# Attention and a Fourier gate on one core: tables from bit operations, transposes in halves, a new order, and matmuls of zeros

## The chip, the core and the metric

The kernel runs on one core of a Trainium2 chip. A core has five engines that work side by side, each through its own list of instructions in order: PE (matrix multiplication, results in the accumulator memory PSUM), DVE (vector work), ACT (functions and copies), POOL (general vector work, and the issue of some transfers) and SP (which only issues transfers). Transfers (DMA) are carried by 16 DMA engines which all queues share. Engines wait for one another through semaphores. The metric is the time of one launch in microseconds (us), the median of several runs; smaller is better.

## The reference

The inputs q, k and v have 8 batches, 8 heads, 576 positions and 64 numbers each. The first stage is a linear attention with a feature map of 2 x 128 features; the second takes its output as `x` (8 x 576 x 512), projects it to three parts, convolves the second over the positions by a Fourier transform, multiplies the three and projects once more.

```python
def phi(x):
    proj = np.einsum('bhsd,df->bhsf', x, w_phi)
    proj = proj - np.max(np.abs(proj), axis=-1, keepdims=True)
    return np.concatenate([np.exp(proj), np.exp(-proj)], axis=-1)
q_p, k_p = (phi(q), phi(k))
kv = np.einsum('bhsf,bhsd->bhfd', k_p, v)
z = np.sum(k_p, axis=2)
num = np.einsum('bhsf,bhfd->bhsd', q_p, kv)
den = np.einsum('bhsf,bhf->bhs', q_p, z)[..., None] + 1e-06
x = num / den                       # heads side by side: 8 x 576 x 512
proj = x @ w_proj                   # 512 x 1536
x1, x2, x3 = proj[..., :D], proj[..., D:2 * D], proj[..., 2 * D:]
X2 = np.fft.rfft(x2, n=S, axis=1)
H = np.fft.rfft(filter_fft, n=S, axis=0)[None, :, :]
x2_conv = np.fft.irfft(X2 * H, n=S, axis=1)
return (x1 * x2_conv * x3) @ w_out
```

## The kernel before

All work is written as a list of words, PLAN (lines 24 to 172), which `run` (line 850) reads from the first to the last. A word is the name of a method, its arguments and, behind `@`, the PSUM bank. `Pk,1,2@0` calls `Pk(1, 2)` on bank 0. Every method issues its instructions on fixed engines, so the order of the words is the order on each engine, and nothing else sets it. Where two engines touch the same buffer, the framework adds the wait. The first number of most words is the batch, 0 to 7. Buffers stand in rings (RING, line 20); two batches of q, k and v fit at once.

One batch takes this way. `load` (line 473) brings q, k or v from memory through POOL's queue, changing float32 to bf16. `tr` (line 485) transposes k or q with a DMA from SP; for batch 0 `loadh` and `trh` (lines 479 and 489) do it in halves. `Pk`, `Qn` and the tails `Pkt`, `Qnt` multiply with `w_phi` on PE (lines 504 to 529), `maxk` and `maxq` take the largest absolute value on DVE (line 576), `ex` the exponentials on ACT (line 560). For q the maxima are cut into a bf16 part (`mhi` on ACT) and the rest (`mlo` on DVE, line 601), transposed (`trm`, line 605, into `mT`) and subtracted within `Pq` by matmuls with the table `sel` (line 543). `em` and `vs` (lines 610 and 616) scale v on POOL, `KV` and `NE` (lines 631 and 652) are the two products of the attention on PE, `rc` and `xn` divide on DVE (lines 666 and 671), and `trx` and `trxt` (lines 690 and 695) transpose the result from SP into `xT` and `xTt`.

From `xT` the second stage begins: `X1` and `X3` (line 750) are projections on PE, as are `X1t` and `X3t` for the tail. `fold` and `foldt` (lines 707 and 713) add and subtract halves of the positions on POOL, `X2` (line 719) projects them, `F` (line 408) is the forward transform as matmuls with the table `fwd`, `m1`, `m2` and `m3` multiply with the filter's transform (tables `A`, `B`), `I` (line 798) is the inverse transform with the table `inv`, `ym` multiplies the parts, `O` (line 830) is the last projection and `st` stores from SP. While one batch is in the second stage the next is in the first; PLAN interleaves them.

Ahead of that the first batch needs tables. The angles of the Fourier tables come from rows that POOL's `iota` writes (`gen_rows`, line 271) and DVE's constants (`gen_phase`); 30 float32 matmuls turn them into columns (`gen_cols`, lines 312 and 314), DVE makes angles of them (`gen_angles`, lines 332 to 335), ACT sines (`gen_sin`). DVE writes the five-part tables (`gen_five`, line 353), `sel` (`gen_sel`, lines 465 to 469) and `inv` (`gen_inv`). Six DMA transposes (`gen_fwd`, line 363) make `fwd`, `fwd5` and `fwdh`. The filter is loaded in 20 pieces from SP (`filt_load`, lines 383 and 385), folded on POOL (`filt_fold`, lines 390 to 393), and `H` with `H_ev` makes `A` and `B`.

The DMAs of a queue share eight semaphores in turn: a DMA on SP waits until the one eight places before it on SP has landed, and so on POOL's queue. POOL waits in its place in the list, so the vector work behind a waiting load waits too.

Of the kernel before, what the change touches and what calls it, by code (L numbers as in the profile page):

```python
# [25 lines left out]
gen_sin loadh,k,0,0 filt_load,SP,0 w_load,phi w_phi trh,q,0,1 Qn,0,3@0 trh,q,0,0 hold,q,0 trh,k,0,0
trh,k,0,1 Qn,0,2@2 maxq,0,2@2 load,k,1 maxq,0,3@0 Qn,0,1@4 maxq,0,1@4 Pk,0,0@2 ex,k,p,0,0@2 Qn,0,0@6
Pk,0,2@0 ex,k,p,0,2@0 ex,k,m,0,2@0 filt_load,SP,1 Qnt,0@4 maxqt,0@4 maxq,0,0@6 Pk,0,1@4 ex,k,p,0,1@4
zeros mhi,0 ex,k,m,0,0@2 gen_selidx gen_five gen_sel Pkt,0@6 exkt,p,0@6 exkt,m,0@6 gen_fwd,3
load,v,0 gen_fwd,0 mlo,0 maxk,0,2@0 trm,0 Pk,0,3@0 load,q,1 ex,k,p,0,3@0 ex,k,m,0,3@0 maxk,0,0@2  # L30
Pq,0,2@2 maxk,0,1@4 ex,k,m,0,1@4 maxkt,0@6 em,p,0,0 em,m,0,0 maxk,0,3@0 tr,k,1 em,p,0,1 gen_fwd,1
Pq,0,1@4 load,v,1 filt_fold H,3@0 H_ev,DVE,3@0 Pq,0,0@6 ex,q,m,0,1@4 ex,q,p,0,1@4 ex,q,p,0,0@6
ex,q,m,0,0@6 H,0@1 H_ev,DVE,0@1 vs,p,0,0 em,m,0,1 ex,q,p,0,2@2 vs,m,0,0 vs,m,0,1 Pq,0,3@4 Pqt,0@0
tr,q,1 KV,0,0@6 KVe,DVE,0,0@6 exqt,p,0@0 gen_inv exqt,m,0@0 NE,0,0@6 rc,0,0@6 ex,q,m,0,2@2 Pk,1,2@0
xn,0,0@6 Pkt,1@2 exkt,p,1@2 exkt,m,1@2 Pk,1,3@6 maxk,1,2@0 ex,q,m,0,3@4 maxkt,1@2 maxk,1,3@6
gen_fwd,5 ex,q,p,0,3@4 em,m,1,1 vs,p,0,1 KV,0,1@2 ex,k,p,1,2@0 KVe,DVE,0,1@2 gen_fwd,2 NE,0,1@4
w_load,proj,0 rc,0,1@4 xn,0,1@4 ex,k,m,1,2@0 w_load,proj,1 gen_fwd,4 ex,k,p,1,3@6 vs,m,1,1 NE,0,2@2
rc,0,2@2 xn,0,2@2 NEt,0@4 rct,0@4 w_load,proj,2 Qn,1,1@0 maxq,1,1@0 xnt,0,1@4 w_load,proj,3 NE,0,3@2
xnt,0,0@4 trxt,0 Qnt,1@0 em,p,1,1 rc,0,3@2 xn,0,3@2 Pk,1,1@4 ex,k,m,1,3@6 ex,k,m,1,1@4 Qn,1,2@6
maxq,1,2@6 H,2@2 H_ev,ACT,2@2 maxqt,1@0 H,1@3 trx,0,3 vs,p,1,1 Qn,1,0@6 maxq,1,0@6 H_ev,ACT,1@3  # L40
trx,0,1 maxk,1,1@4 Qn,1,3@0 trx,0,2 H_fix H,4@2 H_ev,ACT,4@2 maxq,1,3@0 late foldt,0,1 KV,1,1@6
ex,k,p,1,1@4 Pk,1,0@2 X3t,0@4 trx,0,0 X1t,0@5 X1te,ACT,0@5 foldt,0,0 X2,0,4@0 X3,0,3@5 X1,0,3@1
mhi,1 KVe,DVE,1,1@6 mlo,1 maxk,1,0@2 em,p,1,0 load,k,2 X2e,ACT,0,4@0 em,m,1,0 trm,1 X1,0,2@6
X1e,ACT,0,2@6 fold,0,1 X2,0,2@0 X2e,DVE,0,2@0 load,q,2 tmt,0@4 X2,0,3@7 ex,k,p,1,0@2 load,k,3
X2e,DVE,0,3@7 X1,0,1@6 X1,0,0@4 X1e,DVE,0,0@4 ex,k,m,1,0@2 X1e,ACT,0,1@6 F,0,3@0 fold,0,0 X2,0,1@6
X1e,ACT,0,3@1 tm,0,3@5 X2e,DVE,0,1@6 Pqt,1@2 X2,0,0@1 exqt,m,1@2 exqt,p,1@2 X2e,DVE,0,0@1 F,0,2@6
Fe,DVE,0,2@6 Pq,1,0@4 ex,q,p,1,0@4 ex,q,m,1,0@4 vs,p,1,0 Fe,DVE,0,3@0 vs,m,1,0 F,0,1@1 Fe,DVE,0,1@1
# [847 lines left out]
```

## Time and profile before

| What | Value |
|---|---|
| median of 3 runs | 376.44 us (373.03 to 376.76) |
| profiled execution, its own time | 378.21 us |
| profiled execution, span | 376.4 us |
| PE busy | 303.6 us, 81% of the span |
| DVE, POOL, ACT busy | 273.8, 241.2, 219.1 us |
| DMA queue of SP and ACT, share of 16 engines | 38.3% |
| DMA queue of POOL, share of 16 engines | 28.4% |
| read from and written to memory | 33.88 and 9.44 MB |

The span runs from the first to the last instruction that the profile shows; the execution's own time is 1.8 us longer. "Busy" counts the time in which an engine had an instruction under way. In the rows that follow, a row of the timeline gives its start, its length, engine, line, operation and tiles, and in brackets how long the engine had stood idle before and what ended that. A row of stretches gives the stretch, its length, the busy time (and number of instructions) of PE, PE's weight loads, DVE, ACT and POOL, the clock granted to PE as a share of full speed, the busy share of the DMA engines and GB/s. A row of the chain gives start, length and what the chain of waits was in. A row of waits names who waited for whom, the total, how often and the longest.

### The profile page before, as it was taken

Reading aid. Unit: us, or ns where it says so; the run is one execution under the profiler, and the core shown is the slowest. Engines: PE = TensorE matmul, PEld = TensorE weight load, DVE = VectorE, ACT = ScalarE, POOL = GpSimd, SP = SyncE. Lnnn points to the kernel's source line nnn. Section 1 sums busy time; section 2 is a strip of 40 time slices with the busy share of each in tenths; the row PEclk is TensorE's granted clock in tenths of the full one; section 3 lists DMA queues with packets and bytes.
Section 4 is the critical chain, followed back from the end, with each engine's and each line's share of the span. In section 5 each row is a group of like instructions: output and inputs, shape, how many; then the busy total and the mean of one; then the engine's idle time right before and its main releaser. Section 6 shows DMA issues by size and latency. Waiting matters only on the chain.

```text
span 376.4 us, 9310 instructions
## 1 busy us (share of the span) xinstructions
PE 303.6 (81%) x3816; PEld 171.1 (45%) x3863; DVE 273.8 (73%) x450; ACT 219.1 (58%) x346; POOL 241.2 (64%) x184
## 2 busy tenths in 40 slices
PE   5230757599939999798699998699897999999993
PEld 5220345335614565355344664247442664564451
DVE  3759678527947899688577799959885798767860
ACT  1153766436736787467456877567674857763342
POOL 5408455296674998687387766783789478856440
PEclk9999988979979999999879999989998999999998
DMA  8998489794998698667949363536706271223226
GB/s 165 179 210 116 78 127 165 118 178 70 147 168 142 108 95 141 140 114 134 186 75 215 73 108 80 99 64 93 152 4 124 51 135 33 60 51 70 57 63 161
DMA packets 82171, 42.82 MB, mean 114 GB/s; under 512 B 63440, under 2 KB 76368, under 8 KB 82128
## 3 DMA queue, kind: packets, MB, share of 16 engines
q1 hardware_dynamic: 68320, 25.97, 38.3%
q0 software_dynamic: 13808, 16.25, 28.4%
q8 instruction: 30, 0.49, 0.5%
q14 instruction: 13, 0.11, 0.1%
HBM read 33.88 MB, written 9.44 MB: 115 GB/s over the span
## 4 chain that ended last, share of the span: by engine, by line
PE 61%; DMA 18%; DVE 11%; issue 4%; SPq 2%; ACT 2%; POOL 0%; DVEq 0%; ACTq 0%; POOLq 0%
PE ps L750 14%; PE ps L719 9%; PE ps L408 8%; PE ps L830 6%; DMA qT<-qn 6%; PE ps L631 5%; DMA xT<-xn 5%; PE ps L652 4%; PE ps L798 4%; DMA kT<-kn 3%; PE ps L543 2%; DMA qn<-in_q_dram 2%; PE ps L537 2%; PE ps L516 2%; DMA mT<-mh 2%
## 5 line engine op out<-in xcount | busy, mean ns | idle before, releaser
L750 PE MATMUL ps<-xT,wproj 128*128 128x512 bf16 x244 | 69.1, 408 | 10.7 <-DMA xT<-xn 9.8
L576 DVE TENSOR_REDUCE mq<-ps 128x8 f32<-128x1024 f32 (+1 forms) x40 | 43.5, 1111 | 22.8 <-PE ps L523 12.1
L818 POOL TENSOR_TENSOR yT<-cv,x1s 128x576 bf16<-128x576 f32 x25 | 32.4, 1315 | 25.6 <-DVE cv L807 19.1
L616 POOL TENSOR_TENSOR vm<-vn,vm 128x1152 bf16<-128x1152 bf16 x16 | 34.4, 2152 | 20.4 <-ACT vm L610 20.4
L737 POOL TENSOR_TENSOR t<-C,B 128x512 bf16<-128x512 bf16 x32 | 36.4, 1154 | 14.5 <-ACT C L636 7.2
L707 POOL TENSOR_TENSOR eo<-xT 128x1024 bf16<-128x1024 bf16 x16 | 35.0, 2196 | 16.1 <-DMA xT<-xn 9.9
L576 DVE TENSOR_REDUCE mk<-ps 128x8 f32<-128x1024 f32 (+1 forms) x40 | 43.7, 1110 | 2.1 <-PE ps L523 0.6
L616 POOL TENSOR_TENSOR vp<-vn,vp 128x1152 bf16<-128x1152 bf16 x16 | 34.4, 2152 | 12.5 <-ACT vp L610 8.8
L408 PE MATMUL ps<-x2n,fwd 128*128 128x512 bf16 (+1 forms) x121 | 38.2, 387 | 4.7 <-DVE x1s L638 3.0
L750 PEld LDWEIGHTS <-wproj 128*128 128x128 bf16 x256 | 23.6, 103 | 39.0 <-issue 14.6
L560 ACT ACTIVATE Ekp<-ps 128x1024 bf16<-128x1024 f32 x32 | 32.8, 1030 | 14.5 <-PE ps L509 13.2
L830 PE MATMUL ps<-wout,yT 128*128 128x512 bf16 x132 | 36.8, 396 | 3.1 <-ACT x1s L636 1.4
L719 PE MATMUL ps<-wproj,eo 128*128 128x512 bf16 x154 | 39.0, 383 | 0.4 <-issue 0.2
L560 ACT ACTIVATE Eqm<-ps 128x1024 bf16<-128x1024 f32 x32 | 32.4, 1025 | 10.0 <-PE ps L543 10.0
L560 ACT ACTIVATE Eqp<-ps 128x1024 bf16<-128x1024 f32 x32 | 32.9, 1028 | 6.9 <-PE ps L543 6.3
L560 ACT ACTIVATE Ekm<-ps 128x1024 bf16<-128x1024 f32 x32 | 32.8, 1029 | 5.3 <-PE ps L509 4.8
L636 ACT CAST x1s<-ps 128x512 bf16<-128x512 f32 (+1 forms) x32 | 17.2, 547 | 29.7 <-PE ps L750 22.0
L745 POOL TENSOR_TENSOR Y<-Y,t 128x1024 bf16<-128x1024 bf16 x14 | 29.7, 2125 | 2.2 <-DVE Y L733 0.9
L733 DVE TENSOR_TENSOR Y<-ps,A 128x512 bf16<-128x512 f32 x40 | 26.6, 682 | 5.4 <-PE ps L408 5.2
L509 PE MATMUL ps<-wphi,kT 64*128 64x128 bf16 x256 | 14.2, 231 | 18.3 <-DVE mk L576 8.8
L807 DVE TENSOR_TENSOR cv<-es,ps 128x288 f32<-128x288 f32 x64 | 25.4, 447 | 4.2 <-ACT es L802 2.3
L798 PE MATMUL ps<-inv,Y 128*128 128x288 bf16 x192 | 28.3, 291 | 0.0
(142 smaller groups left out, 643.6 us busy)
## 6 DMA issues: line engine op xcount, KB each, us to landing
out_dram<-o SPq DMA_DIRECT2D x72, 128.0 KB, 2.4
vn<-in_v_dram POOLq DMA_DIRECT2D x8, 576.0 KB, 7.3
kn<-in_k_dram POOLq DMA_DIRECT2D x7, 576.0 KB, 8.5
qn<-in_q_dram POOLq DMA_DIRECT2D x7, 576.0 KB, 7.5
wproj<-in_moe_w_proj_dram POOLq DMA_DIRECT2D x4, 384.0 KB, 7.0
fl<-in_moe_filter_fft_dram SPq DMA_DIRECT2D x20, 64.0 KB, 5.2
kn<-in_k_dram POOLq DMA_DIRECT2D x2, 288.0 KB, 5.7
qn<-in_q_dram POOLq DMA_DIRECT2D x2, 288.0 KB, 6.8
```

The source lines that it names most:

```text
L408: self.mm(self.pb(0), l, r, start=(i == 0), stop=(i == len(ks) - 1))
L560: self.nc.scalar.activation(e, self.db(), AF.Exp, bias=0.0, scale=1.0 if g == "p" else -1.0)
L576: self.nc.vector.tensor_reduce(out=out, in_=src, axis=AX.X, op=ALU.max, apply_absolute_value=True)
L616: self.nc.gpsimd.tensor_tensor(out=t[:, :, :, 0:64], in0=self.at("vn", b)[:, 2 * X:2 * X + 2], in1=t[:, :, :, 64:65].to_broadcast([128, 2, ...
L707: self.nc.gpsimd.tensor_tensor(out=o, in0=x[:, :, :, 0, :], in1=x[:, :, :, 1, :], op=op)
L719: self.mm(self.pb(0), eo[:, kt, 128 * c:128 * c + 128], w[:, kt, 512:1024], start=(kt == 0), stop=(kt == 3))
L737: self.nc.gpsimd.tensor_tensor(out=self.at("t2", b)[:, t, :], in0=self.at("C", b)[:, t ^ 1, :], in1=self.at("B")[:, t, :], op=ALU.mult)
L745: e.tensor_tensor(out=Y, in0=Y, in1=self.at("t2", b)[:, s, :], op=ALU.add)
L750: self.mm(self.pb(0), w[:, kt, f0 + 128 * m:f0 + 128 * m + 128], x[:, kt, :], start=(kt == 0), stop=(kt == 3))
L798: self.mm(self.pb(e, 0, 288), Y[:, t, 128 * m:128 * m + 128], inv[:, e, i, :], start=(i == 0), stop=(i == 2))
L818: e.tensor_tensor(out=self.at("yT", b)[:, m, 0:SEQ], in0=self.at("cv", 4 * b + m).rearrange("p j h t -> p (j h t)"), in1=self.at("x1s", b) ...
L830: self.mm(self.pb(0), y[:, kt, 128 * j:128 * j + 128], w[:, kt, :], start=(kt == 0), stop=(kt == 3))
```

## The change

Four things are changed, and with them every position in PLAN.

The tables. The 30 matmuls, `gen_phase` and three iotas are gone; two iotas of one column each, shifts and masks on DVE give the columns (`gen_cols`, in two parts). The products of angle and column move from DVE to ACT (`gen_turns`), the reduction to whole turns stays on DVE in two parts. `gen_five`, `gen_sel`, `gen_inv` and the padding zeros move from DVE to POOL. The six transposes for the tables become two (`gen_fwd` with 12 blocks, `gen_fwd5` with 10). The filter's last row is loaded once a half instead of twice; one half goes through POOL's queue, the other through SP's. `mlo` moves to POOL for the batches 1 to 7.

The transposes. k and q of all batches are transposed in two halves by `trh`: 32 DMAs where there were 18.

The weights. `w_proj` is loaded by the three blocks of its columns in the order 2, 0, 1 (x3, x1, x2), where it was by four blocks of rows.

The matmuls of zeros. `warm,n` issues n matmuls of a zero tile with 512 columns into a bank whose content is not used; there are 48 in all: 22, 11, 2, 4, 2, 4, 1 and 2, the last of them in the middle of the second batch.

```diff
-gen_phase loadh,k,0,1 loadh,q,0,1 loadh,q,0,0 gen_rows gen_half gen_cols@0 gen_cols_ev@0 gen_angles
+w_load,phi w_phi zeros loadh,q,0,0 loadh,q,0,1 gen_rows loadh,k,0,0 trh,q,0,0 warm,22@0 Qn,0,0@0
+gen_cols,1 gen_turns,1 gen_cols,0 gen_turns,0 gen_angles,1 Qn,0,1@2 gen_angles,0 maxq,0,0@0
...
+    def warm(self, n):
+        z = self.at("idle")
+        for _ in range(n):
+            self.mm(self.pb(0).rearrange("p (i x) -> p i x", i=4), z,
+                    z.rearrange("p (i x) -> p i x", i=1).to_broadcast([128, 4, 128]), True, True)
...
-        g.iota(fr[:, 0:4, :], pattern=[[1, 2], [0, 2], [2, 128]], base=0, **kw)
+        g.iota(part, pattern=[[0, 1]], base=0, channel_multiplier=1, **kw)
+        g.iota(even, pattern=[[0, 1]], base=0, channel_multiplier=2, **kw)
...
+        for i in range(3):
+            v.tensor_scalar(out=bit[:, i:i + 1], in0=self.part, scalar1=4 + i, scalar2=1,
+                            op0=ALU.logical_shift_right, op1=ALU.bitwise_and)
+        v.tensor_scalar(out=bit[:, 3:4], in0=self.part, scalar1=15, scalar2=None,
+                        op0=ALU.bitwise_and)
+        v.tensor_copy(fb, bit)
...
+    def gen_turns(self, i):
+        cols = self.at("cols")
+        for t in (range(0, 4), range(4, 7))[i]:
+            self.nc.scalar.activation(self.turn[:, t, :], self.sc, AF.Identity,
+                                      bias=cols[:, 8 + t:9 + t], scale=cols[:, t:t + 1])
+
+    def gen_angles(self, i):
+        v = self.nc.vector
+        r = (slice(0, 4), slice(4, 7))[i]
+        t, w = self.turn[:, r, :], self.whole[:, r, :]
+        v.tensor_copy(w, t)
+        v.tensor_tensor(out=t, in0=t, in1=w, op=ALU.subtract)
...
     def gen_five(self):
-        v, m = self.nc.vector, self.at("msk")
+        g, m = self.nc.gpsimd, self.at("msk")
...
-    def gen_fwd(self, t):
...
+    def gen_fwd(self):
+        self.nc.sync.dma_start_transpose(
+            out=self.at("fwd").rearrange("p t c x -> p (t c) x"),
+            in_=self.G.rearrange("p t x -> p (t x)"))
...
     def gen_inv(self):
-        v, inv, m = self.nc.vector, self.at("inv"), self.at("msk")
+        v, inv, m = self.nc.gpsimd, self.at("inv"), self.at("msk")
...
-        q = self.nc.sync if eng == "SP" else self.nc.scalar
+        q = dict(SP=self.nc.sync, ACT=self.nc.scalar, POOL=self.nc.gpsimd)[eng]
...
-        for e in range(2):
-            q.dma_start(out=self.fl[i][32 * e:32 * e + 32, 2, :], in_=rows[8])
-
-    def filt_fold(self):
+        q.dma_start(out=self.fl[i][0:32, 2, :], in_=rows[8])
+
+    def filt_fold(self, i):
...
-            g.dma_start(out=self.at("wproj")[:, kt, :],
-                        in_=self.dram["w_proj"][128 * kt:128 * kt + 128, :])
+            c = slice(512 * kt, 512 * kt + 512)
+            g.dma_start(out=self.at("wproj")[:, :, c],
+                        in_=self.dram["w_proj"][:, c].rearrange("(t p) f -> p t f", p=128))
...
     def gen_sel(self):
-        v, idx = self.nc.vector, self.selidx
+        g, idx = self.nc.gpsimd, self.selidx
...
+    def gen_selx(self):
+        self.nc.gpsimd.tensor_copy(self.at("sel"), self.one[:, 0, :].rearrange(
...
-    def mlo(self, b):
+    def mlo(self, eng, b):
...
+        e = self.nc.vector if eng == "DVE" else self.nc.gpsimd
+        e.tensor_tensor(out=m[:, :, 1, 0:18], in0=self.at("mq", b),
+                        in1=m[:, :, 0, 0:18], op=ALU.subtract)
```

Three places show how the order moves. On DVE, near the first maxima of q and k, this stood before; `selone` and `sel` are the steps of the table `sel`, `mh` is the parted maximum that `trm` transposes, `mk` the maxima of k:

```order
L355 TENSOR_SCALAR G_154<-g_156,msk_74 128x32
L465 TENSOR_SCALAR selone<-selidx 128x18 x4
L467 TENSOR_TENSOR selone<-selone 128x36
L468 TENSOR_TENSOR selone<-selone 128x18
L469 CAST sel_63<-selone 128x2304
L601 TENSOR_TENSOR mh_88<-mq_86,mh_88 128x2x18
L576 TENSOR_REDUCE mk_84<-ps 128x2x4 x3
```

On DVE the same place now begins with the two parts of the angles and holds nothing of `sel` or of the five-part table `G`:

```order
L352 CAST whole<-turn 128x864
L353 TENSOR_TENSOR turn<-turn,whole 128x864
L352 CAST whole<-turn 128x1152
L353 TENSOR_TENSOR turn<-turn,whole 128x1152
L599 TENSOR_REDUCE mq_86<-ps 128x2x4 x3
L599 TENSOR_REDUCE mq_86<-ps 128x2x2
L599 TENSOR_REDUCE mq_86<-ps 128x2x4
L599 TENSOR_REDUCE mk_84<-ps 128x2x4
L625 TENSOR_TENSOR mh_88<-mq_86,mh_88 128x2x18
```

What moved is the building of `G` and `sel`, which has left the place between the maxima of q and `mh`.

On POOL, from the loads of batch 1 to the first scaling of v (`vp`, `vm`), this stood before:

```order
L474 DMA kn_78<-in_k_dram 128x4x576
L458 IOTA selidx 128x18
L474 DMA vn_79<-in_v_dram 128x4x576
L474 DMA qn_76<-in_q_dram 128x4x576
L474 DMA vn_80<-in_v_dram 128x4x576
L390 TENSOR_TENSOR fe<-fl_203,fl_204 128x512
L391 TENSOR_TENSOR fe<-fl_203,fl_204 128x512
L393 TENSOR_TENSOR fe<-fl_203,fl_204 32x512
L390 TENSOR_TENSOR fe<-fl_203,fl_204 128x512
L391 TENSOR_TENSOR fe<-fl_203,fl_204 128x512
L393 TENSOR_TENSOR fe<-fl_203,fl_204 32x512
L616 TENSOR_TENSOR vp_103<-vn_79,vp_103 128x18x64
```

On POOL now, behind nine pieces of the filter and the eight instructions of `gen_five`:

```order
L485 TENSOR_SCALAR selone<-selidx 128x18 x4
L487 TENSOR_TENSOR selone<-selone 128x36
L488 TENSOR_TENSOR selone<-selone 128x18
L497 DMA vn_79<-in_v_dram 128x4x576
L492 COPY sel_63<-selone 128x2304
L497 DMA kn_78<-in_k_dram 128x4x576
L497 DMA qn_76<-in_q_dram 128x4x576
L640 TENSOR_TENSOR vp_103<-vn_79,vp_103 128x18x64
L640 TENSOR_TENSOR vm_117<-vn_79,vm_117 128x18x64
L640 TENSOR_TENSOR vp_104<-vn_79,vp_104 128x18x64
L519 COPY junk_71<-qT_81 1x1
L640 TENSOR_TENSOR vm_118<-vn_79,vm_118 128x18x64
```

The filter's six folds (`fe`) now stand behind the scaling of v, the loads of batch 1 behind `sel`, and the load of v for batch 1 (`vn_80`) has gone further down.

On SP, from the transposes of k of batch 0 to the first `xT`, this stood before:

```order
L490 DMA_TRANSPOSE kT_82<-kn_77 128x9x128 x2
L383 DMA fl_204<-in_moe_filter_fft_dram 32x512 x8
L385 DMA fl_204<-in_moe_filter_fft_dram 32x512 x2
L363 DMA_TRANSPOSE fwd_66<-G 128x3x128 x2
L605 DMA_TRANSPOSE mT_90<-mh_88 128x128
L486 DMA_TRANSPOSE kT_83<-kn_78 128x18x128
L363 DMA_TRANSPOSE fwd_66<-G 128x3x128
L486 DMA_TRANSPOSE qT_81<-qn_76 128x18x128
L363 DMA_TRANSPOSE fwdh_68<-G_154 128x5x128
L363 DMA_TRANSPOSE fwd_66<-G 128x3x128
L363 DMA_TRANSPOSE fwd_67<-G_154 128x5x128
L695 DMA_TRANSPOSE xTt_133<-xnt_129 128x2x128
```

On SP now:

```order
L513 DMA_TRANSPOSE kT_82<-kn_77 128x9x128 x2
L402 DMA fl_142<-in_moe_filter_fft_dram 32x512 x8
L403 DMA fl_142<-in_moe_filter_fft_dram 32x512
L378 DMA_TRANSPOSE fwd_66<-G 128x12x128
L629 DMA_TRANSPOSE mT_90<-mh_88 128x128
L513 DMA_TRANSPOSE kT_83<-kn_78 128x9x128 x2
L383 DMA_TRANSPOSE fwd_67<-G_145 128x10x128
L513 DMA_TRANSPOSE qT_81<-qn_76 128x9x128 x2
L714 DMA_TRANSPOSE xT_131<-xn_128 128x4x128
L719 DMA_TRANSPOSE xTt_133<-xnt_129 128x2x128
L714 DMA_TRANSPOSE xT_131<-xn_128 128x4x128 x3
```

The first half of the filter, which stood at SP's very start, now stands behind the four transposes of batch 0, and the halves of batch 1 and the tables go in fewer, larger DMAs ahead of `xT`.

More of the change, by code (lines that the diff above doesn't have):

```diff
@@ L24 @@
 PLAN = """
-gen_phase loadh,k,0,1 loadh,q,0,1 loadh,q,0,0 gen_rows gen_half gen_cols@0 gen_cols_ev@0 gen_angles
[L26 to L47, printed above, removed]
@@ L216, in alloc @@
         R("junk", [1, 1], BF16)
+        R("idle", [128, 128], BF16)
         R("cols", [128, 16], FP32)
```

437 lines of the change are left out of this document (225 added, 212 removed).

## The prediction, made before the changed kernel ran

> **What bounds the kernel now.** I read the page first. PE is busy longest, but its slices show where it is not:
>
> ```profile
> span 376.4 us, 9310 instructions
> PE   5230757599939999798699998699897999999993
> ```
>
> One digit is 9.4 us. PE is idle or half idle in the first eight slices (75 us), and later in a few single ones. The same by stages, cut at the first matmul of the second stage:
>
> ```profile
> 0.00:74.50 74.50, 34.32 (x558) 25.97 (x561) 50.31 (x91) 34.34 (x52) 34.34 (x39) 0.95 0.92 146
> 74.50:120.00 45.50, 38.70 (x386) 19.44 (x391) 28.20 (x47) 25.47 (x36) 32.48 (x25) 0.86 0.89 140
> 120.00:200.00 80.00, 72.28 (x927) 38.87 (x938) 62.87 (x101) 50.78 (x84) 58.49 (x42) 0.96 0.80 126
> 200.00:300.00 100.00, 90.22 (x1255) 49.59 (x1268) 79.50 (x117) 69.38 (x111) 73.14 (x48) 0.97 0.51 94
> 300.00:376.40 76.40, 68.11 (x700) 37.22 (x708) 52.94 (x95) 39.15 (x67) 42.72 (x30) 0.98 0.38 79
> ```
>
> The first number behind the length is PE. Before 74.5 us it works 34.3 of 74.5, behind it 269.3 of 301.9. So there are two kernels in one: a start that PE does not bound, and a stream that it nearly does. Of the 32.6 us without PE in the stream, the last 6.2 come behind the last matmul, at the end of the chain shown below. The clock (third number from the end) falls to half where PE restarts after a gap. Five such stretches lie in the stream, with 21.1 us of PE work in all; here are one from the start, and the first and the last of the five:
>
> ```profile
> 52.90:59.40 6.50, 4.96 (x116) 4.49 (x116) 4.94 (x9) 5.25 (x9) 3.04 (x3) 0.51 1.20 184
> 74.50:80.15 5.65, 5.63 (x14) 2.07 (x15) 0.00 (x0) 0.30 (x1) 5.51 (x4) 0.50 0.84 133
> ...
> 288.50:291.90 3.40, 3.11 (x15) 1.11 (x17) 1.29 (x2) 2.56 (x3) 3.32 (x3) 0.50 0.03 7
> ```
>
> Half of 21.1 is lost, 10.6. So the span is 74.5 + 258.7 of work at full clock + 10.6 + 26.4 idle + 6.2 = 376.4.
>
> The chain of waits shows what the start hangs on, and the rate of matmuls of 512 columns:
>
> ```profile
> 1.25 0.89 POOL kn L480
> ...
> 13.77 12.17 DMA kT<-kn
> ...
> 67.75 6.71 DMA xT<-xn
> 74.52 5.30 PE ps L750 x12
> ...
> 201.53 1.73 PE ps L750 x8
> ...
> 369.19 2.37 DMA out_dram<-o
> ```
>
> A matmul takes 0.44 at half clock (12 in 5.30) and 0.216 at full (8 in 1.73). The waits of PE in the stream are mostly for transposes, 17.4 us in these four rows:
>
> ```profile
> PE ps L750 <- DMA xT<-xn: 9.8, 3, 4.9
> PE ps L516 <- DMA qT<-qn: 3.6, 1, 3.6
> ...
> PE ps L523 <- DMA qT<-qn: 2.1, 1, 2.1
> PE ps L543 <- DMA mT<-mh: 1.9, 1, 1.9
> ```
>
> **The change, part by part.** The start up to the first `Pq` and `vs`, from the timeline:
>
> ```profile
> 13.68 1.72 DVE L334 CAST whole<-turn 128x2016 int32<-128x2016 f32 x1
> 14.51 1.23 POOL L474 DMA_DIRECT2D vn<-in_v_dram  x1
> 15.40 10.86 SPq L383 DMA_DIRECT2D fl<-in_moe_filter_fft_dram  x8
> 15.43 2.26 DVE L335 TENSOR_TENSOR turn<-turn,whole 128x2016 f32<-128x2016 f32 x1
> 15.73 0.75 POOL L474 DMA_DIRECT2D qn<-in_q_dram  x1
> 17.87 1.46 PE L516 MATMUL ps<-wphi,qT 64*128 64x128 bf16 x24 [7.02 <-DVE wphi L453]
> 18.95 3.49 DVE L576 TENSOR_REDUCE mq<-ps 128x8 f32<-128x1024 f32 x3 [1.14 <-PE ps L516]
> 26.85 1.82 DVE L576 TENSOR_REDUCE mq<-ps 128x4 f32<-128x512 f32 x2 [4.41 <-PE ps L523]
> 28.73 0.52 DVE L353 TENSOR_SCALAR G<-g,msk 128x256 bf16<-128x256 bf16 x1
> 31.80 1.25 POOL L393 TENSOR_TENSOR fe<-fl,fl 32x512 bf16<-32x512 f32 x1
> 33.18 2.37 DVE L469 CAST sel<-selone 128x2304 bf16<-128x2304 f32 x1
> 35.47 1.25 DVE L601 TENSOR_TENSOR mh<-mq,mh 128x36 bf16<-128x36 f32 x1
> 39.04 0.61 PE L537 MATMUL ps<-qT,wphi 64*128 64x512 bf16 x2 [0.52 <-DVE mk L576]
> 41.72 2.15 POOL L616 TENSOR_TENSOR vp<-vn,vp 128x1152 bf16<-128x1152 bf16 x1 [3.72 <-issue]
> ```
>
> And the usual time from issue to landing, by the page:
>
> ```profile
> kn<-in_k_dram POOLq DMA_DIRECT2D x2, 288.0 KB, 5.7
> ...
> xT<-xn SPq DMA_TRANSPOSE x32, 3.1
> ...
> kT<-kn SPq DMA_TRANSPOSE x9, 5.1
> ```
>
> Transfers of batch 0: q's first half is now first in POOL's queue (1.25), and no filter piece is ahead on SP. It lands near 7 (5.7), its transpose near 12 (5.1), and the first `Qn` stands there in place of 17.87, where `wphi` waited for DVE's angles. One transpose of k took 12.17, because four whole loads of the batches 0 and 1 and the filter ran beside it. Those are now issued later; I take k's second half at 18 where it was 26.
>
> DVE: from 28.73 to 35.47, 6.7 us of tables stand ahead of `mlo`; they go to POOL. The columns need some twenty instructions of one to four numbers, 2 to 3 us if each takes a tenth of a microsecond or a little more (an estimate; the shortest row here, 256 columns, is 0.52). The angles take as long as now, 4.0 less the products, which ACT makes. The chain of `wphi`, columns, products and angles ends near 13. Five maxima (3.49 + 1.82) and one of k bring `mlo` to 20, and its transpose to 24. The 30 matmuls that go lay in PE's idle time; what they delayed was this chain.
>
> POOL: ahead of `sel` stand four loads, nine filter pieces (0.75 each, as the load at 15.73), `gen_five` and `gen_sel`. The last five pieces also wait for transfers eight places ahead, to about 13. `sel` has 2304 columns; POOL's nearest row is `vp`, 1152 in 2.15, so at most 4.3, at least DVE's 2.37. That gives 22 to 27, and the first `Pq` at 25 in place of 39. Bounds 22 and 31.
>
> From `Pq` to the second stage it took 35.5 (39.04 to 74.52). Now POOL scales v from about 26 in four steps of 2.15, to 35, then folds the filter, six steps of 1.25, to 43; ACT's exponentials run beside that. `H,1` waits for the folds, and on PE `NE,0,3` stands behind `H,1`: this is what is late next. Behind `NE,0,3`, at 43, come DVE's division, three issues on SP (1.7 each by the last row of this part), and the landing, 3.1 by the median or 6.7 as here. The second stage then starts at 52 to 56. I take 55, since the DMA engines are 0.92 busy in this part. The weights' second block, issued at 43, has 12 us to land; `gen_inv` on POOL (1728 columns, 3.2 at `vp`'s rate) ends at 47, and the table transposes, two in place of six, are issued 20 us ahead of `H`. Bounds 50 and 62: POOL 3 us faster and 4 slower, and the landing 3 us slower.
>
> The matmuls of zeros: 33 of the 48 lie ahead of 15 us. 22 of them cost 4.8 us (at 0.216) to 9.7 (at 0.44). They start behind `wphi`, near 4.5 (2.4, as the last store, is the shortest landing shown), so they end at 9 to 14, against q's landing at 12: nothing, or 2 us, within my bounds. Their gain there is nothing: the 24 matmuls at 17.87 took 0.06 us each, full clock, after 7 us without work. The other 15 (at most 6.6 us, in waits for DVE and ACT) may keep the half clock of 52.9 to 59.4 away, 2.5 us of a stretch that PE does not bound.
>
> Across the boundary: in the new order `KV,1,1` and one `X2` step stand behind the first X1 instead of ahead of it, 2.1 us. The end, behind the last matmul, is as long as now: 6.2.
>
> The stream: idle and half clock cost 26.4 + 10.6 = 37.0. The nearest cause is the queue of SP: a whole transpose holds it, and `xT` stands behind it:
>
> ```profile
> 175.85 7.84 SPq L486 DMA_TRANSPOSE qT<-qn  x1
> 183.79 3.45 SPq L690 DMA_TRANSPOSE xT<-xn  x2
> ```
>
> Halves hold it for less each, and the new order leaves more PE work between a batch's last `NE` and its first X1 or X3: counted with matmul lengths from the trace, 5.5 to 11.3 us (mean 8.5) against 4.2 to 8.7 (6.1). `mlo` leaves DVE, and its 1.25 there was off the path in the stream: nothing. But the second stage starts 20 us sooner, and the loads of the batches 1 and 2 do not. I take 24 for the 37.0, nearer to the row of now than to its end below. Below, 12: the 17.4 us for transposes gone, and most of the half clock behind them. Above, 47: as now, and 10 more for loads that come late.
>
> Sum: 55 + 258.7 + 2.1 + 24 + 6.2 = 346.0, against a span of 376.4. The profiled execution took 378.2 in all; the median of the runs is 376.4. I take the 30.4 off the median: 346.
>
> One rule speaks against the change. Nine filter pieces move to POOL's queue while DVE works on float32 angles. In the rows above the load issued at 14.51, within DVE's conversion, took 1.23 where the next took 0.75: 0.5 us, inside my bounds. The Trainium skill (SBUF — State Buffer, "SBUF: two separate sides") says that a float32 copy on DVE can lock POOL out of a port that they share, so that POOL cannot write a transfer's descriptors until the copy ends. The trace bears this out only in part: the load at 15.73, within DVE's subtraction, was not longer than others.
>
> **The rivals.** The stream stays as it is: the start gains 20 us, but every transpose is missed as now, 55 + 258.7 + 2.1 + 37 + 6.2 = 359. For it: SP's order changes, the DMA engines do not. Against it: the halves and the longer spans above.
>
> The stream becomes clean: the second stage at 52, and 12 in place of 24: 331. Against it: DVE is 79% busy from 120 to 300 and must hit each step.
>
> The DMA engines bind: they are 0.92 busy up to 74.5 and 0.89 up to 120, so the start cannot be shortened freely. The second stage at 62, the stream 40: 369. Against it: a load of v and a third of the weights now come later.
>
> DVE holds POOL: the conversion and the subtraction, 4.0 us in all, are added in full to POOL's path ahead of `sel`: 350. The rule above gives this where it holds throughout.
>
> Slower, by SP's queue: 14 more transposes go through it. If in each of seven batches one is held as at 175.85 and `xT` behind it is late by 5 us, that eats 35 us of the 30.4: 381. It decides from 4.9 us a batch. For it: holds of that length are in the trace. Against it: in the new order most halves stand far ahead of their use.
>
> The zeros do nothing: that is in the sum already.
>
> **How the numbers follow.** My forecast, 346, has 0.5 (its own range 336 to 355). The stream as now 0.18, the clean stream 0.12, POOL held 0.06, the DMA engines 0.08, slower 0.04; 0.02 are left for gains and losses that cancel. The range 331 to 364 leaves out the two upper cases, the cancelling one and half of the clean one: 0.2. A measurement of this kernel tells about 1% from no change, so faster means under 372.7. All cases but the slower and the cancelling one lie there; the DMA-bound one spreads over it by a third: faster 0.91, same 0.04, slower 0.05.
>
> **What would show it.** Right: the first `Qn` by 13, the first `Pq` at 22 to 31, the first X1 on `xT` at 50 to 62, idle and half clock behind it 12 to 36, no load issue on POOL over 1.3 us while DVE makes the angles, `H,1` waiting for the folds. Wrong: the second stage later than 65 (then look at POOL's filter pieces and at `H,1`), or waits for `qT`, `mT` and `xT` in the stream of more than 17.4 us (then at SP's queue).

## The result and the profile after

The changed kernel took 351.55 us (median of four runs, 349.82 to 355.97), the kernel before 375.8 beside it (373.03 to 376.76). The ratio is 0.935 with a 95% interval of 0.926 to 0.944: faster by 6.5%. The prediction said 346, between 331 and 364. The profiled execution took 353.19 us in all, with a span of 351.2. Run again six times beside the experiments, the same kernel lay between 348.88 and 361.65. So totals tell two variants apart only from about 2%; below that the traces have to.

From the page, the span, and the slices of PE (8.8 us each) and of the granted clock:

```profile
span 351.2 us, 9371 instructions
...
PE   4472578996889999999999999799999999999982
...
PEclk9965589999989999999999999899999999999998
```

From the eighth slice on PE is nearly full, but for a 6 and a 7. Before, single slices of 3, 6 and 7 stood in that part. The stages, cut at the first X1 (columns as in the prediction: length, PE, its loads, DVE, ACT, POOL, clock, DMA share, GB/s):

```profile
0.00:65.10 65.10, 38.94 (x498) 21.95 (x501) 32.91 (x67) 37.80 (x56) 45.40 (x67) 0.79 1.01 149
65.10:120.00 54.90, 48.66 (x655) 26.25 (x662) 40.98 (x66) 38.30 (x59) 42.41 (x31) 0.97 1.03 149
120.00:200.00 80.00, 77.39 (x1094) 43.18 (x1102) 68.33 (x108) 58.61 (x95) 65.51 (x49) 1.00 0.87 131
200.00:300.00 100.00, 96.72 (x1211) 52.64 (x1221) 87.11 (x132) 68.73 (x113) 73.01 (x53) 0.98 0.59 102
300.00:351.20 51.20, 43.53 (x397) 22.91 (x401) 28.67 (x57) 20.95 (x37) 25.69 (x20) 0.97 0.35 79
```

Behind 65.1 PE works 266.3 of 286.1 us. The stream ran at half clock in two places instead of five, by the same view with closer cuts:

```profile
98.70:102.25 3.55, 3.18 (x18) 1.34 (x15) 3.55 (x5) 1.14 (x2) 3.53 (x5) 0.53 0.73 111
224.90:228.20 3.30, 3.30 (x17) 1.33 (x14) 2.71 (x4) 2.90 (x4) 2.16 (x2) 0.50 0.64 54
```

Half of the 6.5 us of work there is lost, 3.2. The last matmuls end at 344.9, 6.3 ahead of the end of the span:

```profile
343.66 1.24 PE L854 MATMUL ps<-wout,yT 128*128 128x512 bf16 x5
```

So the terms of the prediction's sum stand against the trace like this:

| Term | Predicted, us | Measured, us |
|---|---|---|
| start of the second stage | 55 | 65.1 |
| PE's work behind it at full clock, moved work among it | 258.7 + 2.1 | 263.1 |
| idle time and half clock in the stream | 24 | 13.5 + 3.2 |
| end | 6.2 | 6.3 |
| sum | 346 | 351.2 |

Two terms were off in opposite directions. The start gained 9.4 us (74.5 to 65.1) where 19.5 were expected; the stream gained 20.3 (37.0 to 16.7) where 13 were. That the sum is off by only 5 us is luck in part: 10.1 us too few at the start and 7.3 too many in the stream nearly cancel. What is left of PE's waits in the stream shows no transpose any more (before, the four shown rows made 17.4 us):

```profile
PE ps L655 <- issue: 2.9, 1, 2.9
PE ps L426 <- DVE x1s L662: 2.1, 1, 2.1
```

The start, by the chain of waits (start, length, what):

```profile
1.25 4.29 DMA qn<-in_q_dram
5.56 11.79 DMA qT<-qn
17.39 1.04 PE ps L539 x16
18.43 4.80 PE ps L279 x11
...
28.66 8.42 DMA mT<-mh
...
41.54 2.18 PE ps L655 x72
...
65.11 1.02 PE ps L774 x4
```

q is there at 5.5, earlier than predicted, but its transpose takes 11.8 us, and the small transpose `mT` 8.4. Together that is 20 of the first 37 us. L279 is the second group of zeros, and it seems to stand on the path. Whether it does, and why the transposes take so long, the experiments had to tell.

### The profile page after: what moved, and what is told of

Read it like the earlier page. It is cut to its first block, busy times and chain, and to the rows that moved or that the text cites. A ratio compares the mean times of both kernels' runs of the same rounds, so it can differ in the third digit from the quotient of the medians.

```text
span 351.2 us, 9371 instructions
## 1 busy us (share of the span) xinstructions
PE 305.2 (87%) x3836; PEld 166.9 (48%) x3881; DVE 258.0 (73%) x426; ACT 224.4 (64%) x355; POOL 252.0 (72%) x217
## 3 DMA queue, kind: packets, MB, share of 16 engines
q0 software_dynamic: 15104, 16.85, 32.7%
## 4 chain that ended last, share of the span: by engine, by line
PE 75%; DVE 10%; DMA 8%; issue 3%; ACT 2%; SPq 0%; DVEq 0%; ACTq 0%; POOLq 0%
PE ps L774 16%; PE ps L743 10%; PE ps L426 9%; PE ps L854 8%; PE ps L822 7%; PE ps L655 5%; PE ps L676 5%; DMA qT<-qn 3%; PE ps L539 2%; DMA mT<-mh 2%; DVE yT L842 2%; DVE mq L599 2%; PE ps L566 2%; PE ps L560 2%; PE ps L781 2%
## 5 line engine op out<-in xcount | busy, mean ns | idle before, releaser
L774 PE MATMUL ps<-xT,wproj 128*128 128x512 bf16 x239 | 64.5, 389 | 1.6 <-DVE xnt L707 0.3
L599 DVE TENSOR_REDUCE mq<-ps 128x8 f32<-128x1024 f32 (+1 forms) x40 | 43.3, 1110 | 12.6 <-PE ps L539 12.1
L842 POOL TENSOR_TENSOR yT<-cv,x1s 128x576 bf16<-128x576 f32 x22 | 27.9, 1278 | 17.9 <-DVE cv L831 14.9
L583 ACT ACTIVATE Ekm<-ps 128x1024 bf16<-128x1024 f32 x32 | 32.7, 1027 | 6.0 <-PE ps L532 4.9
L731 POOL TENSOR_TENSOR eo<-xT 128x1024 bf16<-128x1024 bf16 x16 | 34.1, 2134 | 2.4 <-DMA xT<-xn 2.4
L583 ACT ACTIVATE Ekp<-ps 128x1024 bf16<-128x1024 f32 x32 | 32.7, 1026 | 4.3 <-PE ps L532 2.2
L660 ACT COPY o<-ps 128x512 f32<-128x512 f32 x29 | 17.0, 588 | 27.4 <-PE ps L854 18.8
L811 DVE TENSOR_TENSOR x1s<-ps,x1s 128x512 bf16<-128x512 f32 x32 | 21.8, 687 | 7.8 <-PE ps L774 6.6
```

Source lines behind the costliest of these rows:

```text
L583: self.nc.scalar.activation(e, self.db(), AF.Exp, bias=0.0, scale=1.0 if g == "p" else -1.0)
L599: self.nc.vector.tensor_reduce(out=out, in_=src, axis=AX.X, op=ALU.max, apply_absolute_value=True)
L731: self.nc.gpsimd.tensor_tensor(out=o, in0=x[:, :, :, 0, :], in1=x[:, :, :, 1, :], op=op)
L774: self.mm(self.pb(0), w[:, kt, f0 + 128 * m:f0 + 128 * m + 128], x[:, kt, :], start=(kt == 0), stop=(kt == 3))
L842: e.tensor_tensor(out=self.at("yT", b)[:, m, 0:SEQ], in0=self.at("cv", 4 * b + m).rearrange("p j h t -> p (j h t)"), in1=self.at("x1s", b) ...
```

## The experiments

Each expectation below is the text that was on record ahead of its run. "Second stage" is the first X1 on `xT`.

**No zeros.** All `warm` words are taken out of PLAN.

```diff
-... trh,q,0,0 warm,22@0 Qn,0,0@0
+... trh,q,0,0 Qn,0,0@0
...
```

> All 48 matmuls of zeros are left out; nothing else changes. Theory A: the start hangs on transposes (of q, and of the parted maxima into `mT`), and the zeros only fill waits. The 22 run in PE's first idle time; the 11 stand between the halves of q from 18.36 to 23.23, but `mT` cannot be issued before 28.6 all the same, because the table transpose holds SP until then. So the first `Pq` stays at 36 to 38, the second stage starts at 63 to 67, and the time stays within 3 us of 351.6. Theory B: the zeros earn their place by the clock: without them PE stays at half clock beyond 46.5 into the second stage, which costs half of up to 10 us of work, 355 to 362. Theory C: the 11 lie on the path in full: 347.

Measured: 351.4 us (348.49 to 355.86), ratio to the kernel before 0.941 (0.930 to 0.951). The first `Pq` on `mT` stood at 37.24 (37.12 with zeros), the second stage at 66.53. The zeros cost nothing and bring nothing that can be measured, as Theory A said; B and C fall. What they do to the clock is seen in the changed kernel itself, in the stretches view of their line alone (the first two numbers are PE's, the last three the clock, the DMA share and GB/s):

```profile
4.70:9.40 4.70, 4.67 (x11) 1.64 (x12) 1.00 1.12 168
9.40:12.20 2.80, 2.77 (x12) 1.06 (x10) 1.00 1.29 167
18.40:23.20 4.80, 4.80 (x11) 1.42 (x11) 0.50 1.08 190
```

The first 11 take 0.42 us each, the half clock (although 1.00 is printed), and the other 11 take 0.25. Then PE waits 5 us for q, the clock is lost again, and the second group pays 4.8 us at half clock to win it back for the few matmuls up to about 27. The Trainium skill (TensorE: Matmul & The Clock Gate, "Part 1: The HAM clock gate") says that the half clock is the default, and that it takes at least one window of some 3.4 us of steady work to leave it; 4.7 and 4.8 us here agree with that.

**No second group.** Only `warm,11` is taken out.

```diff
-maxq,0,1@2 loadh,k,0,1 trh,q,0,1 warm,11@4 Qn,0,2@0 ...
+maxq,0,1@2 loadh,k,0,1 trh,q,0,1 Qn,0,2@0 ...
```

> Only the second group, 11 matmuls of zeros ahead of the third quarter of q, is left out. Theory A: the maxima of q come about 4 us earlier (the second half of q's transpose has landed by 19.1), `mlo` near 24 in place of 27.8, but `mT` is issued at 28.6 as now, since the table transpose holds SP: the time stays within 2 us of 351.6. Theory C: the group is on the path to the second stage: 4 us off, 347 to 348.

Measured: 356.76 us (352.18 to 360.0), ratio 0.949 (0.935 to 0.963); second stage at 66.35. Theory C falls. SP's issues in the timeline (start, length):

```profile
22.44 2.40 SPq L378 DMA_TRANSPOSE fwd<-G  x1
24.93 2.05 SPq L629 DMA_TRANSPOSE mT<-mh  x1
```

On PE, the first matmuls on `mT` in the same timeline:

```profile
37.11 0.61 PE L566 MATMUL ps<-mT,sel 64*128 64x128 bf16 x8 [9.52 <-DMA mT<-mh]
```

`mT` was issued 3.7 us earlier, and landed at the same time, after 12.1 us. Theory A had the first `Pq` right for a wrong reason: not SP's hold but what lies ahead in the transfers sets when `mT` is there. Other executions bear this out: in the seven here that have the table and the loads of batch 1 ahead of `mT` (this run, the one without zeros, the changed kernel twice, and the three with k or q whole further down), it was issued between 24.9 and 29.3 us, and the first `Pq` stood between 36.9 and 37.4. Theory A's time, within 2 us of 351.6, did not come: the median lies 5 above it, with runs from 352 to 360.

**`mT` first.** One word moves in PLAN.

```diff
-... ex,k,p,0,3@2 gen_fwd
-exkt,m,0@4 exkt,p,0@4 maxk,0,3@2 em,p,0,1 trm,0 gen_selx ...
+... ex,k,p,0,3@2 trm,0 gen_fwd
+exkt,m,0@4 exkt,p,0@4 maxk,0,3@2 em,p,0,1 gen_selx ...
```

> `trm` of batch 0 is issued ahead of the table transpose with 12 blocks instead of behind it. Theory A: `mT` is issued only 0.7 us earlier (the parted maxima are ready at 27.95), but it no longer shares the DMA engines with the 12 blocks: it lands in 4 to 6 us where it took 8.42, the first `Pq` stands at 32 to 34, the second stage starts 3 to 4 us earlier, 347 to 349. Rival: the loads of batch 1 (1.15 MB issued at 22.8 and 23.6) set the landing, which stays over 7.5: 351.

Measured: 351.5 us (345.15 to 352.8). SP's issues in the timeline:

```profile
25.88 1.15 SPq L629 DMA_TRANSPOSE mT<-mh  x1
27.13 4.02 SPq L378 DMA_TRANSPOSE fwd<-G  x1
```

The first matmuls on `mT`:

```profile
32.32 0.61 PE L566 MATMUL ps<-mT,sel 64*128 64x128 bf16 x8 [2.77 <-DMA mT<-mh]
```

Without the 12 blocks of the table ahead of it, `mT` landed in 6.4 us (4 to 6 were expected), and `Pq` stood 4.8 earlier. The second stage, at 62.79, gained 2.3 of that (3 to 4 were expected). The time of Theory A (347 to 349) lies within the scatter of the runs and isn't shown by the median.

**The filter later.** POOL's nine filter pieces are issued behind the loads of batch 1.

```diff
-filt_load,POOL,1 trh,k,0,1 Pkt,0@4 ...
+trh,k,0,1 Pkt,0@4 ...
...
-load,k,1 load,q,1 vs,p,0,0 ...
+load,k,1 load,q,1 filt_load,POOL,1 vs,p,0,0 ...
```

> The nine filter pieces of POOL's queue move from 5.7 us to behind the loads of batch 1 (near 24 us, in POOL's idle time). Theory A: the 11.8 us that q's transposes took come from the DMA engines' load at that time: without the nine pieces (0.6 MB) they land in 8 to 10, the first `Qn` at 14 to 15.5, the maxima 2 to 3 us earlier; of that the end sees 0 to 2 us, because SP's table transpose then holds `mT`: 350 to 352. Rival: the landing of q's transposes is set by k's loads alone and stays at 11 to 12; then the time stays or rises by up to 2 us, since the pieces now meet `mT`.

Measured: 354.94 us (353.54 to 358.68), ratio 0.954 (0.943 to 0.965). q's two transposes of batch 0 in the view of transfers (median us to landing, first 36 us), in the changed kernel:

```profile
qT<-qn SPq DMA_TRANSPOSE x2, 11.6
```

And with the pieces later:

```profile
qT<-qn SPq DMA_TRANSPOSE x2, 5.6
```

That settles the transposes of q: nine loads of 64 KB on another engine's queue took their landing from 5.6 us to 11.6 (9.3 when the changed kernel was run again). The Trainium skill (DMA: Bandwidth & Descriptors, "Issuing engines are not separate DMA queues") says that transfers run on the same 16 DMA engines whoever issues them; this pair agrees. The first `Pq` came 11 us earlier, and still the second stage began only 3.0 earlier, at 62.08, and waited again for `xT` after two matmuls. From the timeline, on PE:

```profile
26.27 0.61 PE L566 MATMUL ps<-mT,sel 64*128 64x128 bf16 x8 [2.25 <-DMA mT<-mh]
...
62.08 0.59 PE L774 MATMUL ps<-xT,wproj 128*128 128x512 bf16 x2 [0.16 <-DVE mq L599]
64.28 4.04 PE L774 MATMUL ps<-xT,wproj 128*128 128x512 bf16 x18 [1.61 <-DMA xT<-xn]
```

On POOL:

```profile
33.34 0.50 POOL L402 DMA_DIRECT2D fl<-in_moe_filter_fft_dram  x1 [2.72 <-DMA qn<-in_q_dram]
...
34.34 2.16 POOL L640 TENSOR_TENSOR vp<-vn,vp 128x1152 bf16<-128x1152 bf16 x1
```

The last filter pieces waited, eight places behind, for the loads of k and q, and the scaling of v waited behind them on POOL: 34.3, later than the 32.7 of the changed kernel. Theory A held for the landing, which fell even further, and not for the end: POOL and the landing of `xT` gave back most of what the transposes gained. The median, 3.4 above the changed kernel's, lies within the scatter.

**Without two loads.** POOL fills the two buffers of batch 1 with a constant, so k and q of that batch are not the inputs.

```diff
     def load(self, n, b):
+        if b == 1 and n in "kq":
+            self.nc.gpsimd.memset(self.at(n + "n", b), 0.5)
+            return
```

> The loads of k and q of batch 1 are left out; POOL fills the two buffers with a constant instead, at the same place, in its idle time. So q and k of batch 1 are not the inputs. Theory D: the DMA engines bind the start (busy share 1.01 up to 65.1), and `mT`, issued at 28.7, lands 8.4 later because the two loads stand ahead of it: without them it lands in 3 to 5, the first `Pq` stands at 32 to 34 instead of 37.1, the second stage starts 3 to 5 us earlier, 346 to 349. Rival: `mT` waits for the table transposes of SP's own queue, not for the loads: the first `Pq` stays at 36 to 38, 350 to 353.

Measured: 352.64 us (350.69 to 354.44), ratio 0.934 (0.927 to 0.942). The order on SP in the timeline is that of the changed kernel, with the table ahead of `mT`:

```profile
21.96 2.55 SPq L378 DMA_TRANSPOSE fwd<-G  x1
25.41 1.17 SPq L632 DMA_TRANSPOSE mT<-mh  x1
```

On PE:

```profile
31.01 0.61 PE L569 MATMUL ps<-mT,sel 64*128 64x128 bf16 x8 [2.12 <-DMA mT<-mh]
```

`mT` landed in 5.6 us (3 to 5 were expected), and the second stage stood at 60.93, 4.2 earlier: Theory D's order of events. Its time, 346 to 349, did not follow; the rest of the kernel took 291.1 us instead of 286.1. Behind the second stage other executions with the transposes in halves took from 283.9 us (the five edits further down, 346.6 less 62.7) to 291.0 (the changed kernel run again, 356.2 less 65.2), so such a difference needs no edit. Where these 5 us come from is open.

**k and q whole.** The transposes of the batches 1 to 7 are put back into one, at the place of the first half.

```diff
     def trh(self, n, b, X):
+        if b > 0:
+            key = (n, b)
+            self.seen = getattr(self, "seen", set())
+            if key not in self.seen:
+                self.seen.add(key)
+                self.tr(n, b)
+            return
```

> k and q of the batches 1 to 7 are transposed whole again, at the place of the first of the two halves; the new order and all else stay. Theory A (the prediction's reason for the stream): halves hold SP for less each, so without them `xT` and `mT` come late again, and idle time and half clock behind the first X1, now 16.5 us (13.5 and 3.0), rise by 5 to 15 us: 357 to 366. Theory B: the new order alone makes the stream clean (more PE work between a batch's last `NE` and its first X1): idle and half clock stay within 3 us of 16.5, 350 to 355.

Measured: 382.08 us (380.47 to 386.48), ratio to the kernel before 1.012 (1.006 to 1.019). All of the gain is gone. The second stage stood at 71.75, the rest took 306.9, and PE waited for transposes of q, by its waits behind 66 us (line 567 is `Pq`, 546 `Qn`; total, how often, longest):

```profile
PE ps L567 <- DMA qT<-qn: 12.7, 3, 5.5
PE ps L546 <- DMA qT<-qn: 4.5, 2, 3.4
```

But `Pq` of a batch has no reason to wait for `qT`, since `Qn` has read the same tile before it. What it waits for is the q of the next batch. In PLAN `trh,q,3,0` stands ahead of `Pq,2,2` and `Pq,2,3`, which read the other half of the only buffer; a whole transpose at that place overwrites what they still need, and they wait for it and read batch 3. SP's row and PE's:

```profile
117.11 7.62 SPq L509 DMA_TRANSPOSE qT<-qn  x1
126.88 0.61 PE L567 MATMUL ps<-qT,wphi 64*128 64x512 bf16 x2 [4.60 <-DMA qT<-qn]
```

The same stands in PLAN for q of the batches 2, 4 and 7. So this run computes something else, 12.7 us of its waits belong to that, and neither theory can be read from its 382 us.

**Halves in the kernel before.** Each whole transpose becomes two halves at the same place.

```diff
     def tr(self, n, b):
-        self.nc.sync.dma_start_transpose(
-            out=self.at(n + "T", b), in_=self.at(n + "n", b).rearrange("p v j d -> p (v j d)"))
+        for X in range(2):
+            self.trh(n, b, X)
```

> The kernel before with one edit: each whole transpose of k and q becomes two halves, issued one behind the other. Theory A: transfers of half the size let the others through, and idle time and half clock of the stream, 37.0 us, fall by 5 to 10: 366 to 371. Theory B: the order decides, not the size: the sum of what SP issues is the same, the time stays within 4 us of 376.

Measured: 375.44 us (370.86 to 378.02), against 378.09 (368.71 to 382.59) of the kernel before beside it: no difference is shown, as Theory B said. So halves alone bring nothing in the old order. Together with the 382 us this gave Theory E: q's transposed tile has one buffer (k's has two), and a whole transpose must wait until PE has read all of the batch before.

**Only k whole.**

```diff
     def trh(self, n, b, X):
+        if b > 0 and n == "k":
...
```

> The changed kernel with k of the batches 1 to 7 transposed whole, at the place of the first half; q stays in halves. With both whole it took 382 us. Theory E: what the halves give is the buffer: q's transposed tile has one buffer, so a whole transpose must wait until PE has read all of the batch before, and SP stands with `xT` behind it, while a half may be written as soon as its own half is read. k's tile has two buffers, so k whole costs little: 350 to 358. Theory A: the length of the transfer counts, for k as for q: half of the 30 us, 362 to 370.

Measured: 354.2 us (347.75 to 357.96), second stage at 65.3: nothing is lost that the runs could show. Theory A falls for k.

**k and q whole, two buffers for q.** The run of 382 us with one number changed. Each batch's `Pq` now reads its own q again.

```diff
-RING = {..., 'kT': 2, ...}
+RING = {..., 'kT': 2, 'qT': 2, ...}
```

> As the run with k and q whole (382 us), with one edit: q's transposed tile has two buffers instead of one. Theory E (the one buffer, not the length of the transfer, makes a whole q dear): the waits of SP for PE ahead of q's transposes and of PE for `qT` go, and the time falls back to 350 to 358. Theory A (the length of the transfer, or the place of q's transpose in the order): it stays at 370 or above.

Measured: 358.69 us (354.14 to 367.27), second stage at 66.05. The stretch behind the second stage with one buffer:

```profile
71.70:378.60 306.90, 271.57 (x3338) 146.93 (x3380) 225.42 (x361) 186.94 (x300) 206.30 (x151) 0.95 0.63 107
```

With two:

```profile
66.00:354.10 288.10, 267.93 (x3338) 146.28 (x3380) 226.07 (x360) 186.46 (x300) 206.53 (x151) 0.98 0.68 114
```

PE's work is the same within 4 us; 18.8 of the 306.9 are gone, and 5.7 at the start. No row of PE's waits behind 66 names `qT` any more. The median lies 0.7 above the expected 350 to 358, far from the 370 of Theory A. So with two buffers whole transposes cost nothing that the runs could show. What they cost with one buffer, issued behind the last `Pq` of the batch before, no run shows; so Theory E's reason, SP waiting for PE, stays open.

**Four edits together.** No zeros, `mT` first, the filter pieces behind `sel`, and k of batch 2 behind the first `xT`.

```diff
-... gen_selx Pq,0,0@4
+... gen_selx filt_load,POOL,1 Pq,0,0@4
...
-... maxq,1,1@4 load,k,2 em,m,1,0
+... maxq,1,1@4 em,m,1,0
...
-... load,v,1 foldt,0,0 X3,0,2@5 ...
+... load,k,2 load,v,1 foldt,0,0 X3,0,2@5 ...
...
```

> Four edits to the changed kernel: no matmuls of zeros; `trm` of batch 0 ahead of the table transpose; the nine filter pieces of POOL's queue behind the table `sel` and ahead of the loads of batch 1; the load of k for batch 2 behind the first `xT` transposes. Theory D (the DMA engines and their order bind the start): the first `Pq` stands at 25 to 28, POOL scales v from 29 to 31, the folds end at 45 to 47, `xT` lands in 3 to 5 where it took 7.1 with the pieces late alone, and the second stage starts at 58 to 61 in place of 65.1: 344 to 348. Rival: DVE's and POOL's work up to the second stage binds (DVE's maxima of batch 1 stand last ahead of the first X1 now): 63 to 65, 349 to 352.

Measured: 350.7 us (350.28 to 355.39), ratio 0.933 (0.926 to 0.941), the changed kernel's own within the interval. The first `Pq` stood at 26.56 and the second stage at 60.74, both as Theory D said. Its time, 344 to 348, did not come: `xTt` still took 6.1 us to land (50.97 to 57.05), and v of batch 1 11.5.

**The load of v moved as well.** To these four edits a fifth is added.

```diff
-... xn,0,2@0 w_load,proj,2 ...
+... xn,0,2@0 load,v,1 w_load,proj,2 ...
...
-... load,k,2 load,v,1 foldt,0,0 X3,0,2@5 ...
+... load,k,2 foldt,0,0 X3,0,2@5 ...
```

> The combination of four edits once more (no zeros, `trm` first, filter pieces late, k of batch 2 late), and a fifth: the load of v for batch 1 moves from 59 us to 40 us, where the DMA engines were least busy (0.61 of 40 to 50 us in the changed kernel); in the four-edit run it took 11.5 us to land and POOL's scaling of batch 1 waited for it. Theory D: the second stage still starts at 60 to 62, the early stream no longer waits for v, 344 to 348. Rival: the load meets the transposes of q and `xT` instead, the second stage starts at 63 to 65 and the gain is nothing, 350 to 353.

> The changed kernel unchanged, run again beside the others for comparison on the same chip: 349 to 356, as before.

Measured on one chip: 354.41 us for the five edits (348.35 to 365.01, ratio 0.941, 0.928 to 0.954), 357.21 for the changed kernel, a little above what was expected (348.88 to 361.65, ratio 0.940, 0.930 to 0.950). The second stage of the five edits stood at 62.68, between what Theory D and its rival said, and the median lies above both. The medians are 3 us apart and the intervals lie over each other: no version here is shown to beat the changed kernel.

## Why the prediction came out, point by point

**The tables and POOL: right.** The rows are POOL's in the timeline of the changed kernel, like those on PE and SP further down. Columns, products and angles ended at 12.9 (predicted near 13), `sel` at 22.9 (22 to 27), at 2.12 us on POOL, a little under the lower price. A filter piece took 0.50 where 0.75 was set.

```profile
5.69 3.00 POOL L402 DMA_DIRECT2D fl<-in_moe_filter_fft_dram  x6
...
11.48 0.50 POOL L402 DMA_DIRECT2D fl<-in_moe_filter_fft_dram  x1 [1.67 <-DMA kn<-in_k_dram]
...
20.77 2.12 POOL L492 COPY sel<-selone 128x2304 bf16<-128x2304 bf16 x1
...
32.68 2.15 POOL L640 TENSOR_TENSOR vp<-vn,vp 128x1152 bf16<-128x1152 bf16 x1 [8.36 <-ACT vp L634]
...
44.72 4.94 POOL L409 TENSOR_TENSOR fe<-fl,fl 128x512 bf16<-128x512 f32 x4
```

The last three pieces (9.31, 11.48 and 12.09) were issued beside DVE's float32 subtractions and not within its two conversions to int32, and are as short as the others. In other runs a piece met a conversion, and its issue then ended about 0.1 us behind the conversion's end. The longest is in the run without two loads, POOL's row and DVE's:

```profile
11.71 1.02 POOL L402 DMA_DIRECT2D fl<-in_moe_filter_fft_dram  x1 [1.14 <-DMA kn<-in_k_dram]
11.87 0.76 DVE L352 CAST whole<-turn 128x1152 int32<-128x1152 f32 x1 [0.37 <-ACT turn L345]
```

The rule of the Trainium skill (SBUF — State Buffer, "SBUF: two separate sides") on a float32 copy of DVE that locks POOL out agrees with these rows. Its price was some 0.5 us for the longest piece, and nothing in the changed kernel's own trace: the rival "DVE holds POOL", with 4.0 us, did not happen.

**The start: the step that failed.** It is the price of the transposes: "its transpose near 12 (5.1)" and "`mlo` to 20, and its transpose to 24". q's took 11.8 and `mT`'s 8.4, so the first `Qn` stood at 17.4 for 12 and the first `Pq` on `mT` at 37.1 for 25, outside its bounds, like the second stage outside 50 to 62 and just past the 65 that the text named as wrong. The medians of the page are over the whole run, and from 200 us on the DMA engines were 0.38 to 0.51 busy in the kernel before. The filter pieces beside q's transposes (11.6 to 5.6 without them), and the table and the loads ahead of `mT` (8.4 to 6.4 and 5.6, each without one of the two), are shown. That is the rival "the DMA engines bind", to which the text gave 0.08, with a start that was nearer (62) and a stream that was too long (40). Its rows held a warning: up to the second stage the share of the DMA engines times the length was 0.92 x 74.5 = 68.5 us before, and 1.01 x 65.1 = 65.8 after. In 55 us the same product would have needed a share of 1.2. It is not a fixed amount of work, though: the changed kernel run again had 1.10 x 65.2 = 71.7, the one with four edits 1.01 x 60.7 = 61.3.

**Behind `Pq`: the rates right, the wait wrong.** v's scaling (2.15) and the folds took what was set, 7 us later. The folds ended at 49.7, but `H,1` began only at 52.8, behind `NE,0,2`:

```profile
52.82 0.91 PE L426 MATMUL ps<-fe,fwd 128*128 128x512 bf16 x3
```

So "`H,1` waits for the folds" did not come true; the chain runs through `mT`, `Pq`, ACT's exponentials and `KV`. When `Pq` was moved up by 11 us, POOL's loads and scaling, and then `xT`'s landing, stood at nearly the same length: the second stage came 3.0 earlier with the filter late, 4.4 with four edits; with `mT` first, `Pq` came 4.8 earlier and the second stage 2.3.

**The zeros: right result, wrong reason.** "Nothing, or 2 us" holds. But the text took the clock for full at the start, from the row at 17.87 ("full clock, after 7 us without work"). It was half. Groups of eight like matmuls with `wphi`, in the timeline of the kernel before:

```profile
20.23 0.61 PE L509 MATMUL ps<-wphi,kT 64*128 64x128 bf16 x8 [0.90 <-DVE mq L576]
...
51.27 0.40 PE L509 MATMUL ps<-wphi,kT 64*128 64x128 bf16 x8
53.10 0.61 PE L509 MATMUL ps<-wphi,kT 64*128 64x128 bf16 x8 [1.31 <-DVE xn L671]
```

0.61 is the half clock, as at 53.10, where the profile grants 0.51. The second group of zeros also did not lie ahead of 15 us, but at 18.4 to 23.2; `mT`'s landing hid it.

**The stream: right direction, size short by 7.** 24 was taken, 16.7 came, nearer to the lower bound of 12. The reason given was half right: transposes no longer stand in the way of `xT`. That "halves hold it for less each" is not borne out: halves alone gave nothing, k whole cost nothing, and q whole costs nothing either once it has a second buffer. What halves do is let SP write one part of q's only buffer ahead of matmuls that still read the other, as PLAN has it in four batches; a whole transpose can't stand there without a second buffer. The slower rival, 5 us lost a batch to SP's queue, did not come: no wait for `xT` is left. How much of the 20 us the order gives, and how much the earlier transposes of q, stays open: the order before with two buffers for q was not tried, nor the new order with whole transposes behind the last `Pq`, nor `mlo` back on DVE. Nor is the 20 itself fixed: the changed kernel run again took 291.0 us behind its second stage, where this one took 286.1.

**Moved work and end.** 263.1 for 260.8; three of the zeros (0.65 at full clock) lie behind 65.1, the rest of the 2.3 isn't assigned. The end is as predicted.

## What to carry to other kernels

Before a start is forecast shorter, look at the busy share of the DMA engines there: at 0.92 over 74.5 us, a transfer's median time to landing, taken over the whole run, did not hold (11.8 us for 5.1). The product of share and length is a warning and no floor: it was 68.5, and the second stage then began at 65.1, and at 60.7 with four edits. Transposing in halves lets a transpose stand earlier where the target has a single buffer that is still read; with two buffers whole ones did as well here. If an edit of the order makes an engine wait for a tile that should long be there, look first whether it now reads another batch. And test a suspected clock by the length of equal matmuls, not by the printed share alone.

## What the runs showed of the hardware that was not expected

The clock that the profile prints for the first 38 us of the kernel before is not what PE ran at: the matmuls there were as slow as at 0.51 (0.61 us for eight at 20.23, against 0.40 at 51.27). The stretch from 20 to 40 us, with the 1.00 third from the end:

```profile
20.00:40.00 20.00, 4.44 (x58) 3.06 (x58) 15.49 (x26) 8.61 (x11) 8.60 (x6) 1.00 0.94 152
```

One transpose of 32 KB, `mT`, took between 5.6 and 12.1 us to land in the runs shown above, and issued 3.7 us earlier it landed no earlier. The issue itself stretches as well. SP needed 5.11 us for the table transpose in the changed kernel, 3.53 when the same kernel was run again, 4.85 without any zeros and 2.40 without their second group, so the zeros are not what sets it; what does is open. From SP's timeline of the changed kernel:

```profile
23.45 5.11 SPq L378 DMA_TRANSPOSE fwd<-G  x1
28.66 1.18 SPq L629 DMA_TRANSPOSE mT<-mh  x1
```
